# Pairs of the contraction index in the first loads, and a new written-out order of the units, in a fused two-attention kernel

## The chip, the cores and the metric

The kernel runs on one core of one Trainium2 chip. The metric is device time in microseconds (us), the median of several runs. TensorE (PE) does the matrix products, ScalarE (ACT) and VectorE (DVE) move results out of the accumulator banks (PSUM) and do pointwise work, GpSimd (POOL) does masks and copies, and SyncE (SP) issues all DMAs of the program, one after the other.

## The reference

Two attention layers read the same x of 2048 tokens by 512, and a gate mixes them:

```python
g = sigmoid((x * gate_w).sum(-1, keepdims=True))
a = _A_ref(x, mem0, Wq, Wk, Wv, Wo, 32)   # 64 segments of 32 tokens, one after the other
b = _B_ref(x, wq, wk, wv, wo, beta)       # 4 blocks of 512 tokens, 32 heads of 16
return g * a + (1 - g) * b

# _A_ref, for each segment s: 32 heads of 128
h = concatenate([mem, x_segment])         # 8 memory rows and 32 tokens
q, k, v = h @ Wq, h @ Wk, h @ Wv
p = softmax(where(mask, q k^T * scale, -1e9))
o = (p v) @ Wo
mem = o[:8]; outs.append(o[8:])           # the next segment needs mem

# _B_ref, for each block s of one head
o = sg * (phi(q) M / (phi(q) z + 1e-6)) + (1 - sg) * softmax(q k^T * scale + mask) v
M += phi(k)^T v; z += sum of phi(k)
```

## The kernel before, in words

**First stage (0 to about 51 us).** `plan_warm` runs `WARM` = 9 matmuls on zeros (line 509). `plan_loads` requests x in 8 DMAs of 256 KB, the three 512 KB weights of layer B, then small tensors. `x_chunk` turns x with PE transposes (line 573; x is the stationary operand) and copies the result from PSUM into `xT` (helper `evac`, lines 390 on ACT and 392 on DVE). `b_projections` makes layer B's K, Q and V for three of the four blocks (lines 678, 696) and stores them to scratch memory (line 654). Between its pieces, every third piece requests a quarter (1 MB) of layer A's Wk, Wq, Wv. Contraction index 128c+p lies on partition p in chunk c, so a DMA packet of x or of a B weight is one row of 512 bf16, 1 KB. `gate_parts` turns the gate weight with one more transpose.

**Second stage.** `plan_a` runs 16 groups of four segments. A group has a list of units written out in the file (`A_LIST0` to `A_LIST15`); the lists set the order of the instructions on every engine's queue, and all queues are in order. Units of segment r (0 to 3):

- `r.K0x r.K0y` (and Q, V; head half 0 or 1): two halves of a projection, 8 matmuls each on four row groups of the array (line 1281). `r.k0` copies it out, `r.TK0` turns it on DVE.
- `r.S0` scores (lines 1542, 1547), `r.X0` exp on ACT, `r.Y0` mask, `r.M0` sums (line 1577), `r.L0` logarithm and exp on ACT (the reciprocal; lines 1584, 1587), `r.N0` and `r.n0` multiply (lines 1591, 1597), `r.PV0 r.PL0` p times v (lines 1607, 1619), `r.E0a r.E0b` copy out.
- `r.W0a` to `r.W1b`: output projection with Wo (line 1365), 8 matmuls each. `r.H0 r.H1` copy out as float32 (`WF`), `r.F0 r.F1` fold and turn with small float32 matmuls (`fold`, line 1383; the stationary operand is 32 columns of `WF`), `r.hm0 r.hm1` write the memory rows for the next segment, `r.ax0 r.ax1` the token rows to `aT_st`.
- The last 8 tokens of each segment ("left" tokens) of a group are projected together: `KL0x KL0` and so on for the next group, with a prefix `i` for the first group itself. When both V halves are copied out (`VL0e`, `VL1e`, or `iVL0e iVL1e`), `turn_values` stores them to scratch (line 1316) and reads them back in four DMAs that wait for that store (line 1321); `r.PL0` needs them.
- Layer B's attention: `bS` scores (line 909), `bE` exp on ACT with a mask on POOL, `bP` p times v (line 962), `bT` the rest. Layer B's fourth block is projected late: `pj` is half a projection (line 813), `pp` copies out and stores (line 840). After the fourth of the V tiles is projected (the eighth `pj`), four slices of B weights are requested (line 789).
- `wl` requests an eighth of Wo, 512 KB (line 549): two of them for each of `W0a`, `W0b`, `W1a`, `W1b`.
- `of`, `tb`, `tf`: the tail of each group; `tf` turns token rows back with matmuls into PSUM (line 1482).
- A unit's copy goes to ACT or DVE by the table `A_ENG`; a `~` behind the unit swaps the two.

A unit that needs a PSUM bank takes one of eight; it waits until that bank's last reader is done.

## Time and profile before

| what | value |
|---|---|
| median of 3 runs | 845.19 us (843.88 to 845.63) |
| profiled execution, device time | 845.43 us |
| its span, first to last instruction | 843.4 us |
| PE busy | 811.5 us, 96% |
| ACT, DVE, POOL busy | 589.8, 572.0, 284.8 us |
| mean granted PE clock | 0.996 |

The span is the program itself; 2.03 us of the profiled execution lie around it. A chain of waits is read from the top down: start, length, and the engine or DMA that the next piece waited for. In lists of instruction groups the mean of one is its latency, and the busy time counts overlapping ones once.

### The profile page before, as it was taken

Reading aid. Unit: us, or ns where it says so; the run is one execution under the profiler, and the core shown is the slowest. Engines: PE = TensorE matmul, PEld = TensorE weight load, DVE = VectorE, ACT = ScalarE, POOL = GpSimd, SP = SyncE. Lnnn points to the kernel's source line nnn. Section 1 sums busy time; section 2 is a strip of 40 time slices with the busy share of each in tenths; the row PEclk is TensorE's granted clock in tenths of the full one; section 3 lists DMA queues with packets and bytes.
Section 4 is the critical chain, followed back from the end, with each engine's and each line's share of the span. In section 5 each row is a group of like instructions: output and inputs, shape, how many; then the busy total and the mean of one; then the engine's idle time right before and its main releaser. Section 6 shows DMA issues by size and latency. Waiting matters only on the chain.

```text
span 843.4 us, 49436 instructions
## 1 busy us (share of the span) xinstructions
PE 811.5 (96%) x22174; PEld 441.1 (52%) x22174; DVE 572.0 (68%) x1381; ACT 589.8 (70%) x1506; POOL 284.8 (34%) x780
## 2 busy tenths in 40 slices
PE   8997999999999999999999999999999999999997
PEld 4643455555555555555555555555655555555564
DVE  3554457577566767767767777778687787677764
ACT  5545677767777777777677777777767677777544
POOL 3612233333333343333333333333333333434110
PEclk9999899999999999999999999999999999999999
DMA  9996312112002011111012021111112021110111
GB/s 314 419 365 210 73 51 57 54 29 50 28 18 55 24 48 33 46 38 43 19 37 54 20 52 32 47 38 33 36 24 63 18 52 32 36 45 13 33 41 47
DMA packets 84442, 57.50 MB, mean 68 GB/s; under 512 B 55296, under 2 KB 79112, under 8 KB 82696
## 3 DMA queue, kind: packets, MB, share of 16 engines
q1 hardware_dynamic: 84232, 54.36, 21.2%
q8 instruction: 174, 2.85, 1.4%
q14 instruction: 36, 0.29, 0.1%
HBM read 37.14 MB, written 17.20 MB: 64 GB/s over the span
## 4 chain that ended last, share of the span: by engine, by line
PE 85%; ACT 6%; DMA 5%; DVE 2%; issue 1%; SPq 1%; DVEq 0%; POOL 0%; ACTq 0%
PE ps L1281 46%; PE ps L1365 17%; PE ps L1383 3%; PE ps L1607 3%; PE ps L909 2%; PE ps L962 2%; DMA scr_kqd<-stgk 2%; PE ps L1460 2%; PE ps L1542 2%; PE ps L678 1%; PE ps L1577 1%; ACT R_sb L1587 1%; ACT PT L930 1%; DMA Wo_sb<-in_A_Wo_dram 1%; PE ps L813 1%
## 5 line engine op out<-in xcount | busy, mean ns | idle before, releaser
L936 POOL TENSOR_SCALAR_AFFINE_SELECT PT<-PT 128x128 bf16<-128x128 bf16 (+2 forms) x320 | 117.5, 367 | 206.0 <-ACT PT L930 157.7
L930 ACT ACTIVATE PT<-ps 128x512 bf16<-128x512 f32 x320 | 174.9, 610 | 5.4 <-PE ps L909 4.2
L1281 PE MATMUL ps<-Wq_sb,hT 128*32 128x512 bf16 x2048 | 138.1, 383 | 0.4
L1281 PE MATMUL ps<-Wv_sb,hT 128*32 128x512 bf16 x2048 | 138.2, 379 | 0.0
L1281 PE MATMUL ps<-Wk_sb,hT 128*32 128x512 bf16 x2048 | 136.1, 380 | 0.4
L1365 PE MATMUL ps<-Wo_sb,OT_sb 128*32 128x512 bf16 x2048 | 129.9, 381 | 3.9 <-DMA Wo_sb<-in_A_Wo_dram 3.3
L1597 POOL TENSOR_TENSOR P_sb<-P_sb,R_sb 128x64 bf16<-128x64 bf16 x128 | 50.8, 397 | 136.9 <-ACT R_sb L1587 131.1
L390 ACT ACTIVATE OT_sb<-ps 128x320 bf16<-128x320 f32 x170 | 68.7, 435 | 21.8 <-PE ps L1619 20.4
L1281 PEld LDWEIGHTS ps<-Wq_sb,hT 128*32 128x32 bf16 x2048 | 59.1, 97 | 47.0 <-ACT hT L390 2.9
L1281 PEld LDWEIGHTS ps<-Wk_sb,hT 128*32 128x32 bf16 x2048 | 59.4, 97 | 45.8 <-ACT hT L390 2.6
L390 ACT ACTIVATE WF<-ps 128x256 f32<-128x256 f32 x105 | 35.2, 381 | 58.7 <-PE ps L1365 56.4
L1365 PEld LDWEIGHTS ps<-Wo_sb,OT_sb 128*32 128x32 bf16 x2048 | 48.2, 96 | 48.5 <-ACT OT_sb L390 7.5
L1293 DVE STREAM_TRANSPOSE KT_sb<-KN_sb 128x256 f32<-128x256 f32 x128 | 56.5, 441 | 22.2 <-ACT KN_sb L390 19.2
L1293 DVE STREAM_TRANSPOSE QT_sb<-QN_sb 128x256 f32<-128x256 f32 x128 | 56.4, 441 | 22.0 <-ACT QN_sb L390 18.4
L390 ACT ACTIVATE QN_sb<-ps 128x512 bf16<-128x512 f32 x78 | 46.9, 604 | 34.0 <-PE ps L1281 33.3
L390 ACT ACTIVATE KN_sb<-ps 128x512 bf16<-128x512 f32 x75 | 45.0, 602 | 33.2 <-PE ps L1281 32.8
L1556 ACT ACTIVATE P_sb<-ps 128x224 bf16<-128x224 f32 x128 | 45.9, 359 | 28.5 <-PE ps L1547 20.6
L1281 PEld LDWEIGHTS ps<-Wv_sb,hT 128*32 128x32 bf16 x2048 | 50.2, 95 | 23.8 <-issue 0.6
L1591 DVE TENSOR_TENSOR P_sb<-P_sb,R_sb 128x160 bf16<-128x160 bf16 x128 | 42.0, 329 | 20.8 <-ACT R_sb L1587 18.6
L392 DVE CAST V_sb<-ps 128x512 bf16<-128x512 f32 x76 | 51.8, 682 | 5.5 <-PE ps L1281 5.1
L392 DVE CAST OT_sb<-ps 128x320 bf16<-128x320 f32 x86 | 41.1, 487 | 18.7 <-PE ps L1619 17.6
L1607 PEld LDWEIGHTS ps<-P_sb,V_sb 32*128 32x128 bf16 x2048 | 23.4, 91 | 57.6 <-DVE P_sb L1591 26.0
(142 smaller groups left out, 1490.0 us busy)
## 6 DMA issues: line engine op xcount, KB each, us to landing
Wk_sb<-in_A_Wk_dram SPq DMA_DIRECT2D x4, 1024.0 KB, 10.1
Wq_sb<-in_A_Wq_dram SPq DMA_DIRECT2D x4, 1024.0 KB, 13.6
Wv_sb<-in_A_Wv_dram SPq DMA_DIRECT2D x4, 1024.0 KB, 15.4
Wo_sb<-in_A_Wo_dram SPq DMA_DIRECT2D x8, 512.0 KB, 5.7
scr_vld<-VNL SPq DMA_DIRECT2D x16, 256.0 KB, 2.8
VL<-scr_vld SPq DMA_DIRECT2D x64, 64.0 KB
scr_kqd<-stgk SPq DMA_DIRECT2D x12, 256.0 KB, 9.7
Vj<-scr_vd SPq DMA_DIRECT2D x32, 68.0 KB, 2.4
```

Of the source, the lines that this page charges most:

```text
L390: P.op("act", lambda a: a.activation(dst, src, ACT.Copy), reads=[v.rbank[k] for k in bks], writes=dres, name=name)
L392: P.op("dve", lambda d: d.tensor_copy(dst, src), reads=[v.rbank[k] for k in bks], writes=dres, name=name)
L930: P.op("act", lambda a: a.activation(pt, v.pb[bk], ACT.Exp, scale=v.SCALE_B), reads=[v.rbank[bk]], writes=[rp], name="be%d_%d" % (n, t))
L936: P.op("gp", lambda g: g.affine_select(mv, mv, [[0, len(cut)], [1, 128]], ALU.is_ge, 0.0, base=0, channel_multiplier=-1), reads=[rp], writ ...
L1281: ins = pe.matmul(pb[bk][SEG * j:SEG * (j + 1), :], lhs(c), cols(w, j) if split else w[:, 512 * j:512 * (j + 1)], start=(c == 0), stop=(c ...
L1293: P.op("dve", lambda d: d.transpose(to, src), reads=reads, writes=writes, name=name)
L1365: ins = pe.matmul(pb[bk][SEG * j:SEG * (j + 1), :], lhs(4 * k + j), Wo_sb[:, 4 * k + j, :], start=(first and k == ks[0]), stop=False, skip ...
L1383: ins = pe.matmul(pb[bk][SEG * j:SEG * (j + 1), SEG * n:SEG * (n + 1)], part[:, o:o + SEG], v.fold[:, :], start=True, stop=True, skip_grou ...
L1556: P.op("act", lambda a: a.activation(P_sb[:, b, :], pb[bk][:, 0:224], ACT.Exp, scale=SCALE), reads=[rbank[bk]], writes=[Rs("P%d" % b), Rs( ...
L1591: P.op("dve", lambda d: d.tensor_tensor(wide(P_sb, b)[:, :, 0:L], wide(P_sb, b)[:, :, 0:L], R_sb[:, b, :].rearrange("p (i q) -> p i q", q= ...
L1597: P.op(ENG["n"], lambda d: d.tensor_tensor(left(P_sb), left(P_sb), grp04(R_sb[:, b, :]), ALU.mult), reads=[Rs("R%d" % b)], writes=[Rs("P%d ...
L1607: ins = pe.matmul(pb[bks[j]][:, L * i:L * (i + 1)], V_sb[SEG * j:SEG * (j + 1), b, i * E:(i + 1) * E], P_sb[SEG * j:SEG * (j + 1), b, LW * ...
```

## The change

In x, the B weights, A's weights, `gate_w` and the folded outputs, contraction index 256h+2p+n now lies on partition p in chunk 2h+n. A partition then holds two neighbouring rows, and a packet of a B weight is 2 KB; x comes in 2 KB packets (first chunk) or 4 KB packets (the others, one DMA each in place of two). Rows of A's weights stay 8 KB. Operands that run along this index take every second element (`by_pairs`, `a_rows`): the stationary operand of the x transposes and of the folds, the stationary operand and the PSUM destination of `tf`'s matmuls, and the destination of the copies to `aT_st` (units `ax` and `of`). Copies into `xT` write every second or fourth element, and the first chunk's two are split between ACT and DVE in another way. The gate weight arrives in its place, without a transpose. V of a B block is stored once for four tiles (4.25 KB packets) in place of four times. The late slices of the B weights take two DMAs each. `WARM` goes from 9 to 7. All sixteen lists are written anew; every list holds the same projections, scores and outputs as before, and only units of layer B and of the tails change lists. The diff, with lists 1 to 15 and the end of list 0 left out:

```diff
@@ -9,7 +9,7 @@
...
 DEV = dict(nseg_limit=None)
-WARM = 9
+WARM = 7
...
@@ -314,7 +314,7 @@
...
     in_p = alloc(esP, ("wkB", [128, C, DM], BF16, 0), ("wqB", [128, C, DM], BF16, 0), ("phK", [128, 4, DM], BF16, 0), ("etmp", [128, 512], BF16, 5),
-          ("bmask", [128, 136], BF16, 0), ("mskT", [128, 2, 8, 2, 2], BF16, 0), ("mem0_sb", [128, DM], BF16, 0), ("gwr_sb", [128, 128], BF16, 0), ("beta_sb", [128, HB], BF16, 0),
+          ("bmask", [128, 136], BF16, 0), ("mskT", [128, 2, 8, 2, 2], BF16, 0), ("mem0_sb", [128, DM], BF16, 0), ("beta_sb", [128, HB], BF16, 0),
...
@@ -367,7 +367,7 @@
...
-        parts = {"mem0_sb": "mem0", "gwr_sb": "gwr", "beta_sb": "beta", "gB_sb": "gB", "omgB_sb": "omgB"}
+        parts = {"mem0_sb": "mem0", "beta_sb": "beta", "gB_sb": "gB", "omgB_sb": "omgB"}
...
@@ -413,7 +413,7 @@
...
             v.late_const()
-        if n >= 36 and n % 2 == 0 and gates:
+        if n >= 38 and n % 2 == 0 and gates:
...
@@ -514,29 +514,30 @@
...
     P, Rs, C, M = v.P, v.Rs, v.C, v.M
-    xsrc = A_x[0].rearrange("(i p) d -> p i d", p=128)
-
...
     def x(k):
+        if k:
+            P.dma(P.group("x%d" % k), lambda s: s.dma_start(v.x_sb[:, 4 * k:4 * k + 4, :], A_x[0, 512 * k:512 * (k + 1)].rearrange("(p i) d -> p i d", i=4)),
+                  writes=[Rs("x_sb%d%d" % (k, h)) for h in range(2)], name="dma_X%d" % k)
+            return
         for h in range(2):
-            o = 4 * k + 2 * h
-            ld("x%d%d" % (k, h), v.x_sb[:, o:o + 2, :], xsrc[:, o:o + 2, :], "x_sb%d%d" % (k, h), "dma_x%d%d" % (k, h))
+            ld("x%d%d" % (k, h), v.x_sb[:, 2 * h:2 * h + 2, :], A_x[0, 256 * h:256 * (h + 1)].rearrange("(p i) d -> p i d", i=2), "x_sb%d%d" % (k, h), "dma_x%d%d" % (k, h))
...
     for nm, dst, src in (("wk", v.wkB, B_wk), ("wq", v.wqB, B_wq), ("wv", v.wvB, B_wv)):
-        ld("b" + nm, dst[:, :, :], src.rearrange("(c p) n -> p c n", p=128), nm + "B", "dma_" + nm)
+        ld("b" + nm, dst[:, :, :].rearrange("p (h n) m -> p h (n m)", h=2), src.rearrange("(h p n) m -> p h (n m)", h=2, n=2), nm + "B", "dma_" + nm)
...
     for fn, res in ((lambda s: s.dma_start(v.beta_sb[:, :], B_beta.rearrange("(o n) -> o n", o=1).to_broadcast([128, v.HB])), "beta"),
-                    (lambda s: s.dma_start(v.gwr_sb[0:C, :], gate_w.rearrange("(c p) -> c p", p=128)), "gwr"),
+                    (lambda s: s.dma_start(v.gw_sb[:, :].rearrange("p (h n) -> p h n", h=2), gate_w.rearrange("(h p n) -> p h n", h=2, n=2)), "gw"),
...
     def weight(grp, dst, src, res, c):
-        P.dma(grp, lambda s: s.dma_start(dst[:, c, :], src[c * 128:(c + 1) * 128].rearrange("p h e -> p (h e)")),
+        P.dma(grp, lambda s: s.dma_start(dst[:, c, :], src.rearrange("(a p n) h e -> a n p (h e)", a=2, n=2)[c // 2, c % 2]),
...
@@ -558,6 +559,21 @@
...
+def by_pairs(ap):
+
+    return Pairs(ap)
+
+
+class Pairs:
+
+
+    def __init__(self, ap):
+        self.ap = ap.rearrange("p (h t n) -> p h n t", h=2, n=2)
+
+    def __getitem__(self, key):
+        return self.ap[key[0], key[1] // 2, key[1] % 2, key[2]]
+
+
...
@@ -570,14 +586,13 @@
...
                     o = (n * C + c) * 128
-                    ins = pe.transpose(v.pb16[bk][:, o:o + 128], v.x_sb[:, i, c * 128:(c + 1) * 128], v.ident[:, :])
+                    ins = pe.transpose(v.pb16[bk][:, o:o + 128], by_pairs(v.x_sb[:, i, :])[:, c, :], v.ident[:, :])
...
         P.op("pe", f, reads=[Rs("x_sb%d%d" % (k, h)), Rs("ident")], writes=[v.rbank[bk]], name="xtr%d_%d" % (k, h))
-        t0 = 128 * tiles[0]
-        dst = v.xT[:, :, t0:t0 + 256].rearrange("p c (n t) -> p n c t", t=128)
+        dst = v.xT[:, :, 512 * k:512 * (k + 1)].rearrange("p c (t n) -> p n c t", n=4)[:, 2 * h:2 * h + 2] if k else v.xT[:, :, 256 * h:256 * (h + 1)].rearrange("p c (t n) -> p n c t", n=2)
...
         for n in range(2):
-            v.evac("dve" if h else "act", dst[:, n, :, :], src[:, n, :, :], [bk], [Rs("xT%d_%d%d" % (k, h, n))], "xev%d_%d%d" % (k, h, n))
+            v.evac("dve" if (n if k == 0 else h) else "act", dst[:, n, :, :], src[:, n, :, :], [bk], [Rs("xT%d_%d%d" % (k, h, n))], "xev%d_%d%d" % (k, h, n))
...
@@ -599,13 +614,6 @@
...
     st = {}
-
-    def weights():
-        bk = BK.take()
-        P.op("pe", lambda pe, bk=bk: pe.transpose(v.pb16[bk][:, 0:C], v.gwr_sb[0:C, :], v.ident[0:C, 0:C]),
-             reads=[Rs("gwr"), Rs("ident")], writes=[v.rbank[bk]], name="gwtr")
-        v.evac("dve", v.gw_sb[:, :], v.pb16[bk][:, 0:C], [bk], [Rs("gw")], "gwev")
-        BK.give(bk)
...
@@ -630,12 +638,12 @@
...
             for c in range(C):
-                ins = pe.transpose(v.pb16[bk][:, c * v.M:(c + 1) * v.M], v.mem0_sb[0:v.M, c * 128:(c + 1) * 128], v.ident[0:v.M, 0:v.M])
+                ins = pe.transpose(v.pb16[bk][:, c * v.M:(c + 1) * v.M], by_pairs(v.mem0_sb[0:v.M, :])[:, c, :], v.ident[0:v.M, 0:v.M])
...
         BK.give(bk)
-    return [weights, memory] + [lambda k=k: dots(k) for k in range(NTT // 4)]
+    return [memory] + [lambda k=k: dots(k) for k in range(NTT // 4)]
...
@@ -698,8 +706,9 @@
...
         v.evac("act", v.V17[:, sb % 2, tt, :, 0:16].rearrange("p (e m) d -> p m e d", e=2), v.pb[bk].rearrange("p (m e d) -> p m e d", e=2, d=16), [bk], [rv], "evv%d_%d" % (sb, tt))
-        store("stv%d" % sb, v.vd[sb, :, tt, :], v.V17[:, sb % 2, tt, :, :].rearrange("p h w -> p (h w)"), [rv, Rs("V17o")], [Rs("vd%d_%d" % (sb, tt))],
-              "stv%d_%d" % (sb, tt))
+        if tt == 3:
+            store("stv%d" % sb, v.vd[sb].rearrange("p t w -> p (t w)"), v.V17[:, sb % 2, :, :, :].rearrange("p t h w -> p (t h w)"),
+                  [Rs("V17_%d_%d" % (sb % 2, t)) for t in range(4)] + [Rs("V17o")], [Rs("vd%d_%d" % (sb, t)) for t in range(4)], "stV%d" % sb)
...
@@ -784,9 +793,11 @@
...
         m, f = self.work[4 + i]
-        src = (v.B_wk if m == "K" else v.B_wq).rearrange("(c p) n -> p c n", p=128)[:, :, 128 * f:128 * (f + 1)]
-        dst = v.woB_sb[:, i % 4, :].rearrange("p (c w) -> p c w", w=128)
-        P.dma(P.group("lw%d" % i, "lw%d" % (i % 4)), lambda s: s.dma_start(dst, src), writes=[Rs("woc%d" % (i % 4))] + ([Rs("wvB")] if i < 4 else []), name="ldc%d" % i)
+        src = (v.B_wk if m == "K" else v.B_wq).rearrange("(h p n) m -> p h n m", h=2, n=2)[:, :, :, 128 * f:128 * (f + 1)]
+        dst = v.woB_sb[:, i % 4, :].rearrange("p (h n w) -> p h n w", h=2, w=128)
+        grp = P.group("lw%d" % i, "lw%d" % (i % 4))
+        for h in range(2):
+            P.dma(grp, lambda s, h=h: s.dma_start(dst[:, h], src[:, h]), writes=[Rs("woc%d" % (i % 4))] + ([Rs("wvB")] if i < 4 else []), name="ldc%d_%d" % (i, h))
...
@@ -1033,214 +1044,213 @@
 
 
 A_LIST0 = """
-    ixl iKL0x iQL0x iQL0 iQL1x iQL1 iKL0 pj iKL1x iKL0e iKL1 wl 0.Q1x 0.Q1y iQL1e pj 0.K0x 0.K0y 0.q1 0.TQ1 iQL0e~ iKL1e~ bS wl bE iVL0x 0.V0x bE 0.V0y bE
-    0.xc bE 0.Q0x 0.v0~ pp 0.Q0y 0.q0 0.TQ0 bS bP wl bP 0.qt 0.k0~ 0.TK0 pj bE pj wl bE 0.S0 0.X0 iVL0 iVL1x iVL1 0.K1x wl 0.K1y iVL0e~ bE 0.Y0 0.M0 pj xl
-    pp 0.k1 iVL1e bE wl 0.L0 wl 0.TK1 bP wl 0.S1 0.X1 bS 0.Y1 bP bE bE pj bE KL0x 0.M1 0.n0 bE 0.L1 pp 0.V1x 0.V1y 1.xc QL0x 0.v1 QL0 QL0e~ QL1x QL1 bP
-    0.N1 VL0x VL0 0.N0 QL1e~ bT 0.n1 KL1x KL1 VL1x VL0e bP KL0 VL1 KL1e~ 0.PV0 0.PL0 pj VL1e~ 0.E0b~ 0.E0a 0.PV1 0.PL1 0.E1a~ 0.E1b~ KL0e 0.W0a 0.W0b bS
-    pj bE bE bE 0.W1a 0.W1b 0.H0 0.F0 0.oL 0.H1 0.F1 0.hm1~ 1.qt 0.hm0 pp 1.Q1x 1.Q1y 1.Q0x 1.Q0y bE 1.q0 1.TQ0 1.K0x 1.q1 1.TQ1 1.K0y 1.k0 1.TK0 1.K1x
...
+    0.K1x 0.K1y 0.K0x pj 0.k1 wl 0.Q1x ixl iQL1x iKL0x iKL0 iQL1 0.Q0x 0.Q0y 0.q0~ 0.K0y wl iQL1e~ iKL0e~ 0.TK1 bS pj 0.Q1y bE bE bE iVL1x wl 0.k0~ 0.TK0
+    bE bS 0.xc bP iVL1 bP 0.q1 0.TQ1 bE bE pp wl bE bE iVL0x iVL0 wl 0.TQ0 iVL0e~ iKL1x iKL1 iKL1e~ iQL0x iQL0 iQL0e xl pj pj wl 0.qt bP KL0x KL0 KL1x pp
+    0.V0x iVL1e wl 0.V0y 0.v0~ KL1 wl 0.S0 VL1x KL0e~ bP 0.X0 VL1 KL1e~ bS pj 0.Y0 bE QL1x QL1 bE bE 0.S1 0.X1 pj bE pj pj bP 0.Y1 0.M1 QL1e~ pp 0.M0 0.L1
+    0.N1 VL0x VL0 0.L0 0.n0 bT 0.V1x 0.V1y QL0x QL0 VL0e~ 1.xc VL1e~ 0.v1~ 0.N0 0.PV0 0.PL0 0.E0b 0.E0a~ QL0e~ bP 0.W0a 0.n1 0.PV1 0.PL1 0.E1b~ 0.E1a~
+    0.oL 1.qt 0.W0b bS bE bE 0.W1a bE 0.W1b 0.H0 0.F0 bE 0.hm0 0.H1~ 0.ax0 0.F1 1.Q1x 1.Q0x 0.hm1~ 1.Q0y 1.q0~ 1.TQ0 1.Q1y pp 1.K0x 1.K0y 1.k0~ 1.TK0
...
     """
...
@@ -1379,14 +1389,18 @@
...
                 for j in range(4):
-                    o = 256 * hf + 128 * n + SEG * j
-                    ins = pe.matmul(pb[bk][SEG * j:SEG * (j + 1), SEG * n:SEG * (n + 1)], part[:, o:o + SEG], v.fold[:, :],
+                    cols = by_pairs(part[:, :])[:, 2 * hf + n, SEG * j:SEG * (j + 1)]
+                    ins = pe.matmul(pb[bk][SEG * j:SEG * (j + 1), SEG * n:SEG * (n + 1)], cols, v.fold[:, :],
...
         return pb[bk][:, 0:2 * SEG].rearrange("p (c t) -> p c t", t=SEG)
+
+    def a_rows(t):
+
+        return t[:, :, :].rearrange("p c t -> p (c t)").rearrange("p (a t c) -> p a t c", a=2, c=2)
...
@@ -1420,7 +1434,7 @@
...
             n = 3 if g == ngrp - 1 else 4
-            dst = aT_st[par][:, :, :].rearrange("p (a c) (r t) -> p a c r t", a=2, t=SEG)[:, :, :, 0:n, SEG - 8:SEG]
+            dst = a_rows(aT_st[par]).rearrange("p a (r t) c -> p a c r t", t=SEG)[:, :, :, 0:n, SEG - 8:SEG]
...
@@ -1441,7 +1455,7 @@
...
         last = g == ngrp - 1
-        rows = aT_st[g % 2] if last else aTg
+        rows = a_rows(aT_st[g % 2] if last else aTg)
...
@@ -1479,7 +1493,7 @@
...
                         q = slice(SEG * j, SEG * (j + 1))
-                        ins = pe.matmul(pb[bk][q, c * 128:(c + 1) * 128], rows[:, c, q], ident[:, :], start=True, stop=True)
+                        ins = pe.matmul(by_pairs(pb[bk][q, :])[:, c, :], rows[:, c // 2, q, c % 2], ident[:, :], start=True, stop=True)
...
@@ -1654,14 +1668,14 @@
...
             if last:
-                dst = aT_st[par][:, :, SEG * r:SEG * (r + 1)].rearrange("p (a c) t -> p a c t", a=2)
+                dst = a_rows(aT_st[par])[:, :, SEG * r:SEG * (r + 1), :].rearrange("p a t c -> p a c t")
...
                 return
-            dst = aT_st[par][:, :, SEG * r:SEG * (r + 1) - M].rearrange("p (a c) t -> p a c t", a=2)
+            dst = a_rows(aT_st[par])[:, :, SEG * r:SEG * (r + 1) - M, :].rearrange("p a t c -> p a c t")
...
```

## The prediction

> **What bounds the kernel.** I read the page first, then windows of time, then the chain of waits.
>
> ```profile
> span 843.4 us, 49436 instructions
> PE 811.5 (96%) x22174; PEld 441.1 (52%) x22174; DVE 572.0 (68%) x1381; ACT 589.8 (70%) x1506; POOL 284.8 (34%) x780
> ...
> PEclk9999899999999999999999999999999999999999
> ```
>
> PE is the bound; only its 31.9 us of idle time, time at a low clock and work added to it can move the end. In the windows of 10 us (columns: length, then busy time of PE, PEld, DVE, ACT, POOL, then granted clock, DMA share, GB/s) idle time and clock loss sit together:
>
> ```profile
> 50.00:60.00 10.00, 9.88 (x176) 4.94 (x176) 5.39 (x12) 3.37 (x7) 1.14 (x4) 1.00 1.01 346
> 60.00:70.00 10.00, 7.88 (x208) 4.03 (x212) 4.23 (x9) 8.02 (x18) 3.81 (x11) 1.00 0.92 300
> 70.00:80.00 10.00, 8.26 (x184) 3.54 (x176) 7.32 (x17) 5.22 (x11) 2.69 (x8) 1.00 0.58 180
> 80.00:90.00 10.00, 7.06 (x104) 2.88 (x108) 1.64 (x4) 2.98 (x7) 1.58 (x4) 0.66 0.52 136
> ```
>
> Summing such windows, PE idles 11.0 us before 100, 14.6 from 100 to 800, 6.3 after. The chain names the cause near 80 (start, length, what):
>
> ```profile
> 65.60 5.72 DMA scr_vld<-VNL
> ...
> 73.88 0.60 SPq L549
> ...
> 75.08 7.29 DMA Wo_sb<-in_A_Wo_dram
> ...
> 82.41 1.07 PE ps L1365 x5
> ...
> 84.69 5.56 PE ps L1281 x63
> ...
> 162.74 3.43 PE ps L1281 x64
> ```
>
> SP stores the first left values at 65.60, waits 5.3 us for them to land, reads them back until 73.84, and only then issues the last three Wo requests, which five others preceded. PE idles 3.26 us before 82.41. Then 63 matmuls take 5.56 us where 64 take 3.43 at full clock: 2.1 us more.
>
> **The start.** (Timeline; the bracket is idle time before.)
>
> ```profile
> 1.26 4.02 PE L509 MATMUL ps<-WF 128*128 128x512 bf16 x9 [1.26 <-DVE WF L503]
> 5.08 1.85 PE L573 MATMUL ps<-ident,Wo_sb 128*128 128x128 bf16 x16
> 7.77 1.04 PE L678 MATMUL ps<-xT,wkB 128*128 128x512 bf16 x4 [0.85 <-DVE xT L392]
> 9.08 1.04 PE L678 MATMUL ps<-xT,wqB 128*128 128x512 bf16 x4 [0.27 <-DMA wqB<-in_B_wq_dram]
> ```
>
> Warm matmuls start 0.43 us apart (PEld rows), so two fewer bring the transposes 0.85 forward, to 4.2. The fastest x transfer took 2.8 us from its issue at 0.81, so x is there. wk landed at 7.3 (issue 1.82 plus 5.5). From 2 to 8 us, with 1 KB packets alone, DMA moved 282 to 336 GB/s; from 20 to 40, mostly 8 KB rows, 415 to 423. The 1 MB up to wk takes about 0.9 less at the higher rate: 6.4, before the first projection is due at 6.9. The copy on DVE loses speed by its 4 or 8 byte steps: from 0.42 (xT copy) to at most 0.69 (the float32 cast of the same shape), but the first chunk is now split over both engines, so I put it at nothing. The wq wait of 0.27 goes. The first 16 transposes took 1.85 us where a later 16 take 1.06: PE was still slow until about 7; a projection that starts sooner may run slow, +0.2. Sum: -0.9 (bounds 0 and -1.3).
>
> Up to 51 us PE is full but for 0.85 in 40 to 50 and 0.72 at 50.05 (waiting for ACT's copy of V, itself late after 2.5 us of waiting for a store of 256 KB that took 15 us to land behind the backlog). 3.6 MB of x and B weights at 415 instead of about 310 GB/s are 2.9 us less DMA time, and V's stores go from twelve to three. I take -0.6 of that idle time (bounds 0 and -1.5). The gate transpose (0.17) goes: -0.1. Together -1.6.
>
> **Group 0.** I add PE time along the lists: 0.43 us per half projection (8 of the 64 matmuls in 3.43), 0.1 to 0.4 for the small units, as the chain shows them. Both lists hold 58.2 us. `iVL1e`, which releases the store, stands at 13.4 before and 13.5 after, and `0.W1b`, the last user of Wo, at 24.6 in both. So the Wo requests do not move by PE time; what changes is SP's queue. Six requests instead of five stand ahead of the store. The first was issued at 57.92, long after its place (3.9 into a list that began at 51.1), because four V stores (3.62 us on SP from 53.78) and MZ's store stood ahead; now one store does, and the backlog is 2.9 us shorter. The six (3.1 MB at the 300 to 340 GB/s of that stretch, 9 to 10 us) should be through by 66. The values' store, issued about 65, lands by 69; reading back takes 2.5; two requests go out by about 72.6. Three took 7.3 from the last issue; two at about 330 GB/s should need 5, so 77.6. `0.W1b` is due at 49.5 + 24.6 + some 3 us of other waits = 77.1. Residual wait: 0.6 (bounds 0 and 3.3). A short wait need not cool the clock. Gain: 3.3 + 2.1 - 0.6 = 4.8.
>
> New waits in group 0: the second `bS` stands at 7.0 and needs four banks; the pending late tile, Q half 1 and VL half 1 hold three, so it takes banks that the four `bE` behind copies on ACT free at about 8.9: near 2 us. PE stands in it with everything behind. Before, the same stretch had 0.8 (a DVE copy), 1.0 (POOL's mask) and 0.4 (a late store's source); I set these against it: 0, bounds -1 and +1.5. The late slices take eight DMAs more on SP, 0.5 us each. Four of these come before group 1's values, whose first reader is a segment away; cover gone, 2 us. I put it at nothing.
>
> **Groups 1 to 15.** The lists are the same work in another order. For each of the 64 segments and both halves I took the PE work between producer and consumer and compared it with the chain between: sums to PV (0.31 + 0.34 + 0.34 and hand-overs, 1.3), PL to W (0.47 + 0.2), W to fold (0.55), fold to the next projection (0.4), projection to scores (0.62 + 0.45 + 0.25), scores to sums (0.9). The shortfalls add up to 30.3 us before and 30.05 after, for groups 1 to 15 26.1 and 26.2; only group 14 (-0.7) and group 15 (+0.7) differ much. Before, 21 us were really idle from 100 on, so the count is of the right size, and says nothing changes: 0, bounds -3 and +3, for the waits on ACT that it leaves out. The last tail still starts after the last `ax1`: 0.
>
> **Operands with steps.** No row shows the folds' float32 columns 8 bytes apart. The nearest has bf16 4 bytes apart (L1542, keys), which loads as fast as contiguous columns:
>
> ```profile
> L1542 PEld LDWEIGHTS ps<-QT_sb,KT_sb 128*32 128x32 bf16 x2048 | 31.9, 95 | 28.2 <-DVE QT_sb L1293 10.5 <-DVE KT_sb L1293 8.2 <-issue 1.2
> L1383 PEld LDWEIGHTS ps<-fold,WF 128*32 128x32 f32 x2048 | 30.9, 111 | 22.4 <-ACT WF L390 9.2 <-DVE WF L392 2.0 <-issue 1.6
> L1482 PE MATMUL ps<-ident,aTg 128*32 128x128 bf16 x240 | 6.3, 219 | 0.3 <-issue 0.3
> ```
>
> I take 0 for the folds; the upper end is a doubled load, 15 ns (30.9/2048) times 2560, 38 us. The x transposes likewise: 0, at most their 4.7 us of loads again. For L1482, whose result now falls on every second float32 of PSUM, rows give 0 to +3.4: 128 columns on four row groups at 0.43 ns a column (from the two L1577 shapes, 42 ns for 96 columns) are 0.21 us a tail, doubled, 16 times. I take 0.
>
> The Trainium skill speaks against this edit (Advanced Engine Details and Errata, PSUM Cachelines): any non-contiguous access pattern "significantly slows down matmuls". No row here shows single elements with gaps; L1577's 64-column form, in runs of eight, runs at full rate.
>
> **Sum.** -1.6 - 4.8 = -6.4 on the profiled 845.43 (span 843.4 and 2.03 around it) is 839.0; the median lies 0.24 lower: 838.8. Bounds of the forecast's own parts: 834 to 843.5.
>
> **Rivals.**
> - *The last Wo requests come no sooner* (0.14). For it: they still queue behind the read-back of the values, at the same place by PE time. Against it: two instead of three, and a shorter backlog. Then only the start and about 1 us are gained: 842.5.
> - *PSUM steps double `tf`* (0.06): 838.8 + 3.4 = 842.2.
> - *The new order loses on ACT and DVE* (0.10), which my count leaves out: `~` moves copies, and a copy behind a row of `bE` (0.5 to 0.6 each) makes PE wait. Place: groups 1 to 15. At 0.6 us a group it costs 9: 847.8; it decides from 0.43 a group on. Against it: ACT is at 70%, DVE at 68%.
> - *The folds' 8 byte steps slow the weight load* (0.07): 160 folds of 16 loads. At 0.1 us a fold, 16 us: 854.8, slower; it decides from 0.04 us a fold (6.4/160). Against it: L1542.
> - *Gains and losses cancel* (0.06), the first two together with a bad half microsecond here and there: 845.
>
> **How the numbers follow.** The forecast has 0.57. About 0.2%, 1.7 us, is what a measurement of this kernel can tell from no change. Faster: 0.57 + 0.14 + 0.06 = 0.77; same 0.06; slower 0.17. The range goes from 832.5, a little under the forecast's own end since the start's idle time could go wholly, to 848, which takes in the order's loss and leaves out the folds' case.
>
> **What would show it.** Right: the first L678 near 6.9; no half clock in 80 to 90; PE's wait for Wo under 1.5 us; three V stores from the first stage in place of twelve; folds' load mean at 111 ns, L1482 at 219; idle time from 100 to 800 between 12 and 18. Wrong: the Wo wait still at 3, a PEld mean of L1383 well above 111, or idle time from 100 on above 24.

## The result and the profile after

The changed kernel is slower by 0.7%: 851.16 us (median of 4 runs, 849.22 to 852.74) against 845.18, ratio 1.0066, interval 1.0044 to 1.0089. The prediction was 838.8, faster. The profiled execution is the fastest of the four (849.22; before 845.43), so its trace shows 4.1 us of span out of some 5.6 by the ratio.

The page of the changed kernel, to be held against the one of before:

```profile
span 847.5 us, 49417 instructions
PE 814.6 (96%) x22165; PEld 439.3 (52%) x22171; DVE 569.8 (67%) x1366; ACT 602.4 (71%) x1520; POOL 285.0 (34%) x780
...
PEclk9999999999999999999999999999999999999999
```

PE is still the bound, and of the 4.1 us it is busy for 3.1 more. The slice at the low clock has gone, as forecast. The windows from 50 to 90 (length; busy PE, PEld, DVE, ACT, POOL; granted clock; DMA share; GB/s) show the half clock of 80 to 90 gone (1.00 instead of 0.66), but PE idle for 1.97 us in 50 to 60, where it idled 0.12 before, and hardly more work done by 90:

```profile
50.00:60.00 10.00, 8.03 (x136) 3.99 (x138) 2.56 (x7) 3.76 (x7) 0.00 (x0) 1.00 1.05 372
60.00:70.00 10.00, 8.73 (x173) 3.79 (x168) 3.73 (x10) 7.16 (x15) 3.66 (x12) 1.00 0.74 246
70.00:80.00 10.00, 8.64 (x228) 3.83 (x220) 4.68 (x13) 7.93 (x19) 3.24 (x7) 1.00 0.55 161
80.00:90.00 10.00, 7.12 (x160) 2.96 (x160) 3.77 (x9) 4.67 (x12) 2.44 (x6) 1.00 0.66 185
```

The chain of waits in the same stretch (start, length, what):

```profile
69.12 5.90 DMA scr_vld<-VNL
75.03 0.53 SPq L1331
...
77.57 0.60 SPq L550
78.22 5.14 DMA Wo_sb<-in_A_Wo_dram
83.40 0.65 PE ps L1375 x8
...
86.51 2.64 DMA scr_vd<-t_sb
89.17 0.63 ACT t_sb L390
89.80 0.48 ACT QN_sb L390
90.32 0.61 PE ps L1291 x8
```

The values are stored at 69.12 instead of 65.60 and the last piece of Wo is there at 83.40 instead of 82.41. PE's wait for it is short (0.74 instead of 3.26) mainly because PE itself comes late. Then a second chain takes over: a store of late values goes out at 86.51, ACT may write `t_sb` again only when it has landed (89.17), and a projection behind ACT's next copy waits until 90.32.

The start (timeline; idle time before in brackets):

```profile
1.26 3.17 PE L509 MATMUL ps<-WF 128*128 128x512 bf16 x7 [1.26 <-DVE WF L503]
4.22 1.62 PE L589 MATMUL ps<-ident,Wo_sb 128*128 128x128 bf16 x16
5.32 1.33 ACT L390 ACTIVATE xT<-ps 128x512 bf16<-128x512 bf16 x2 [3.23 <-PE ps L589]
6.10 1.33 DVE L392 COPY xT<-ps 128x512 bf16<-128x512 bf16 x2 [4.89 <-ACT xT L390]
7.88 1.02 PE L686 MATMUL ps<-xT,wkB 128*128 128x512 bf16 x4 [2.04 <-DMA wkB<-in_B_wk_dram]
9.14 1.89 PE L686 MATMUL ps<-xT,wqB 128*128 128x512 bf16 x4 [0.23 <-DMA wqB<-in_B_wq_dram]
```

The transposes come at 4.22 as forecast, but the first projection starts at 7.88 instead of 7.77: PE now waits 2.04 us for wk, and from 9.14 on four matmuls take 1.89 us instead of 1.04; the granted clock in 10 to 12 is 0.50. List 0 begins at 52.6 instead of 51.1. Only 0.1 us of this is the later projection. The rest is the half clock: from the first projection to list 0 it takes 44.7 us here, 43.3 before, and 43.2 in e6, which has the same loads and no fall of the clock.

The copies into `xT` are slower too. Before, they read:

```profile
6.17 1.08 ACT L390 ACTIVATE xT<-ps 128x512 bf16<-128x512 bf16 x2 [4.09 <-PE ps L573]
6.96 0.76 DVE L392 COPY xT<-ps 128x512 bf16<-128x512 bf16 x2 [5.76 <-PE ps L573]
```

Into every second element one copy now takes 0.73 us on ACT and 0.72 on DVE, instead of 0.59 and 0.42, and DVE's first one begins only when ACT's first one has ended. They are done at 7.43, not far ahead of wk.

The operands with steps (groups: busy, mean ns of one):

```profile
L1393 PEld LDWEIGHTS ps<-fold,WF 128*32 128x32 f32 x2048 | 31.0, 112 | 22.0 <-ACT WF L390 8.8 <-DVE WF L392 2.4 <-issue 1.6
L1496 PEld LDWEIGHTS ps<-ident,aTg 128*32 128x32 bf16 x240 | 6.1, 116 | 2.2 <-issue 0.7 <-DVE V_sb L392 0.2
L1496 PE MATMUL ps<-ident,aTg 128*32 128x128 bf16 x240 | 9.5, 303 | 0.2 <-issue 0.2
```

The folds' 8-byte steps cost nothing (112 ns against 111). The tail's matmuls into every second word of PSUM take 303 ns instead of 219, and their weight loads 116 instead of 96.

To place the differences, the table takes three marks of each trace: the start of the last matmul of unit `W` from `OT_sb` in segments 1 and 59, and the end of the span. All figures are differences to the trace of before (96.34, 791.52, 843.38), and the last two columns are the stretches between the marks. Such a mark of a single execution is uncertain by 2 us and more. Up to segment 1 the change, e2, e5 and e11 run the same instructions and stand between -0.20 and +2.37, and so do e3, e8 and e10, between -0.63 and -2.84: in e2 the clock was at half from 8 to 14 us, in e3 it fell once in 80 to 90 (0.83 there). From segment 1 to 59 the change, e1, e5, e6 and e11 are alike and lose 2.36 to 3.95. So the medians and their ratios decide, and the marks only show where to search.

| kernel | segment 1 | segment 59 | end | 1 to 59 | 59 to end |
|---|---|---|---|---|---|
| the change | -0.05 | +2.59 | +4.13 | +2.64 | +1.54 |
| e1, 9 warming matmuls | +0.74 | +3.10 | +6.78 | +2.36 | +3.68 |
| e2, PSUM in a row, DVE in halves | +2.37 | +4.58 | +6.12 | +2.21 | +1.54 |
| e3, new lists alone | -0.63 | +0.73 | +3.76 | +1.36 | +3.03 |
| e4, loads and pairs alone | +3.54 | +5.32 | +5.40 | +1.78 | +0.08 |
| e5, last list of before | -0.20 | +2.94 | +3.19 | +3.14 | +0.25 |
| e6, 12 warming matmuls | -0.29 | +3.66 | +5.42 | +3.95 | +1.76 |
| e7, three parts mended | -1.34 | +1.47 | +1.03 | +2.81 | -0.44 |
| e8, before with new lists 0 to 2 | -2.84 | -2.98 | -2.78 | -0.14 | +0.20 |
| e9, e8 with two requests a slice | -2.11 | -2.23 | -1.87 | -0.12 | +0.36 |
| e10, e8 with PSUM steps | -2.54 | -0.51 | -0.17 | +2.03 | +0.34 |
| e11, one block of the last list moved | +0.11 | +3.34 | +5.94 | +3.23 | +2.60 |
| e12, before with new lists 3 to 14 | +0.30 | +1.91 | +1.68 | +1.61 | -0.23 |

### The profile page after: what moved, and what is told of

It is laid out like the page before. It is cut to its first block, busy times and chain, and to the rows that moved or that the text cites. A ratio compares the mean times of both kernels' runs of the same rounds, so it can differ in the third digit from the quotient of the medians.

```text
span 847.5 us, 49417 instructions
## 1 busy us (share of the span) xinstructions
PE 814.6 (96%) x22165; PEld 439.3 (52%) x22171; DVE 569.8 (67%) x1366; ACT 602.4 (71%) x1520; POOL 285.0 (34%) x780
## 4 chain that ended last, share of the span: by engine, by line
PE 85%; ACT 6%; DVE 3%; DMA 2%; issue 1%; POOL 1%; SPq 0%; DVEq 0%; POOLq 0%
PE ps L1291 44%; PE ps L1375 17%; PE ps L1393 4%; PE ps L1621 3%; PE ps L920 3%; PE ps L973 2%; PE ps L686 2%; PE ps L1474 2%; ACT PT L941 2%; PE ps L1556 1%; PE ps L1591 1%; PE ps L704 1%; DMA wqB<-in_B_wq_dram 1%; ACT R_sb L1601 1%; PE ps L1496 1%
## 5 line engine op out<-in xcount | busy, mean ns | idle before, releaser
L1291 PE MATMUL ps<-Wq_sb,hT 128*32 128x512 bf16 x2048 | 135.9, 380 | 0.2
L1611 POOL TENSOR_TENSOR P_sb<-P_sb,R_sb 128x64 bf16<-128x64 bf16 x128 | 51.5, 402 | 154.6 <-ACT R_sb L1601 150.7
L390 ACT ACTIVATE OT_sb<-ps 128x320 bf16<-128x320 f32 x180 | 72.0, 434 | 25.6 <-PE ps L1633 23.9
L1291 PEld LDWEIGHTS ps<-Wk_sb,hT 128*32 128x32 bf16 x2048 | 57.4, 97 | 46.1 <-ACT hT L390 3.0
L390 ACT ACTIVATE QN_sb<-ps 128x512 bf16<-128x512 f32 x90 | 54.3, 604 | 29.1 <-PE ps L1291 28.4
L392 DVE CAST V_sb<-ps 128x512 bf16<-128x512 f32 x79 | 53.7, 682 | 2.8 <-PE ps L1291 1.9
L392 DVE CAST KN_sb<-ps 128x512 bf16<-128x512 f32 x51 | 34.5, 676 | 23.2 <-PE ps L1291 23.0
```

The source lines that it names most:

```text
L390: P.op("act", lambda a: a.activation(dst, src, ACT.Copy), reads=[v.rbank[k] for k in bks], writes=dres, name=name)
L392: P.op("dve", lambda d: d.tensor_copy(dst, src), reads=[v.rbank[k] for k in bks], writes=dres, name=name)
L1291: ins = pe.matmul(pb[bk][SEG * j:SEG * (j + 1), :], lhs(c), cols(w, j) if split else w[:, 512 * j:512 * (j + 1)], start=(c == 0), stop=(c ...
L1611: P.op(ENG["n"], lambda d: d.tensor_tensor(left(P_sb), left(P_sb), grp04(R_sb[:, b, :]), ALU.mult), reads=[Rs("R%d" % b)], writes=[Rs("P%d ...
```

## The experiments

Times are medians; a ratio is to the kernel before, run on the same chip beside it (845.52 us for e1 to e4, 845.76 for e5 to e8, 846.47 for e9 to e12), so kernels of different sets are compared by their ratios. 0.1% is 0.85 us.

**e1: nine warming matmuls in the changed kernel.**

```diff
-WARM = 7
+WARM = 9
```

> The changed kernel with WARM back at 9 and nothing else undone. Theory A (its loss is a sum: a colder start, tf's steps in PSUM, and small waits of the new lists): two more warm matmuls shorten PE's idle stretch before the first projection from 2.0 to about 1.2 us, the granted clock of 0.94 and 0.89 in the first 20 us goes back to 1.00, and list 0 starts 1.5 to 2 us sooner: 849 us. Theory B (the new order alone is what costs): the start is absorbed by later waits and the time stays at 851. Theory C (the packets of 2 KB land later and that alone makes the start late): first projection still at 7.9, time within 0.5 of 851.

852.13 us, ratio 1.0078 (1.0052 to 1.0104): nothing gained. The transposes start at 5.08 as before the change, PE still waits 2.06 us for wk, and the clock in 10 to 12 is 0.51. wk simply landed later here, at 8.1.

**e2: the tail's transposes into consecutive words of PSUM.** The step moves to the one DVE operation behind them, which then needs two halves.

```diff
-  pe.matmul(by_pairs(pb[bk][q, :])[:, c, :], rows[:, c // 2, q, c % 2], ident[:, :], ...)
+  pe.matmul(pb[bk][q, c * 128:(c + 1) * 128], rows[:, c // 2, q, c % 2], ident[:, :], ...)
...
-  scalar_tensor_tensor(fin, pb[bk], g, t1)              # one of 512
+  for each half: scalar_tensor_tensor(fin[half, step 2], pb[bk][half], g, t1[half, step 2])
```

> The changed kernel with tf's matmuls writing each chunk contiguously into PSUM; the step of two is taken by the DVE that reads it, in two instructions of 256 columns instead of one of 512. Theory A: the matmul's mean goes from 303 back to 219 ns and its busy time from 9.5 to 6.3 us, PE is the bound there, so 3.4 us come off: 847.8. Theory B: the matmul gets faster and the time does not, since other waits take the place: 851. A DVE that becomes late would show as a wait of PE for it, and less gain than 2 us.

The matmuls are back at 219 ns (6.3 us busy), but the time is 851.36, ratio 1.0074 (1.005 to 1.0097), no better than the change's 1.0066. DVE has more to do for it: 32 operations of 477 ns in place of 15 of 738 and two of 478, 3.2 us more. That this used up the gain is likely and was not tried apart; from segment 1 to 59 the trace loses 2.21, hardly less than the 2.64 of the change. So this run did not show what the PSUM step costs by itself; e10 does.

**e3 and e4: the two halves of the change apart.**

```diff
# e3: the kernel before
-A_LIST0 ... A_LIST15   (before)
+A_LIST0 ... A_LIST15   (of the change)
# e4: the changed kernel
-A_LIST0 ... A_LIST15   (of the change)
+A_LIST0 ... A_LIST15   (before)
```

> The kernel before with the sixteen new lists and nothing else of the change. Theory A: the wait for Wo shrinks from 3.3 to under 1.5 us and the half clock after it goes (4.7 us), the new waits at the head of list 0 cost about 3, groups 1 to 15 cost 0 to 2: 843 to 846. Theory B: the order is what costs, 849 to 851.

> The changed kernel with the sixteen old lists: pairs, longer packets, WARM 7, tf in steps. Theory A: start 1.5 late (2.5 with the clock), tf 3.4 more, the wait for Wo as before: 849 to 851. Theory B: with the old order the time is that of before, 845, or less by what the shorter DMA backlog saves.

New lists alone: 847.66, ratio 1.0032 (1.0015 to 1.0049). Loads and pairs alone: 849.58, ratio 1.0058 (1.0039 to 1.0076). Both lose. In the table the loads lose 3.54 us by segment 1, with PE's wait for Wo still 3.4; the lists are ahead at segment 1, by 0.63 in spite of a fall of the clock there, and lose 3.03 after segment 59.

**e5: the last list of before in the changed kernel.**

```diff
-A_LIST15   (of the change)
+A_LIST15   (before, its leading tf as bT)
```

> The changed kernel with the last group's list (A_LIST15) as before; its leading tf, which has nothing to do here, becomes a bT. Theory (the new last list opens idle places of PE near the end, 1.5 to 2 us between 820 and 828 us that no later work can take up, and in some runs a fall of the clock behind them): 1.5 to 3 us less than the changed kernel, 848.2 to 849.7, and from the end of segment 59 to the end about 51.9 us as before instead of 53.4. Rival (the last group's order is neutral, and what is lost there only shows up there since it was owed by earlier groups): within 0.7 us of the changed kernel, 850.5 to 851.9.

847.71, ratio 1.0016 (1.0005 to 1.0027), 0.5% or 4.2 us better than the change by the ratios, more than expected. In the traces the eight kernels with the last list of before (the kernel before itself among them) need 51.4 to 52.2 us from segment 59 to the end, the six with the new one 53.4 to 55.5. Timeline of PE in the changed kernel, segment 62:

```profile
824.01 0.28 PE L1591 MATMUL ps<-P_sb,onesb 128*32 128x160 bf16 x8 [0.29 <-DVE P_sb L1574]
824.61 0.46 PE L1393 MATMUL ps<-fold,LN_sb 128*32 128x32 f32 x32 [0.32 <-DVE V_sb L392]
825.57 0.28 PE L1621 MATMUL ps<-P_sb,V_sb 32*128 32x40 bf16 x16 [0.49 <-DVE aT_st L392]
...
826.44 0.27 PE L1621 MATMUL ps<-P_sb,V_sb 32*128 32x40 bf16 x16 [0.57 <-ACT OT_sb L390]
```

Four waits for copies on DVE and ACT in 2.5 us; before, the same stretch of segment 62 had one, 0.64 us. In some executions the clock falls behind them. The window in e3 (same list, columns as above):

```profile
825.00:830.00 5.00, 5.00 (x96) 2.30 (x92) 0.79 (x3) 1.39 (x4) 0.40 (x1) 0.72 0.22 53
```

e1 has 0.77 there, the change's own profiled execution 1.00. That fits its times: the mean granted clock over the whole span was 0.998 in its two faster executions (849.22 and 850.65 us) and 0.996 in the two slower ones (851.67 and 852.74), and one more stretch at half clock as long as the one at the start (3.4 us, 8.8 to 12.2) makes 0.002 of such a span. Where in the span the clock fell in the other three is not on record. Where the clock holds there, the new list costs 1.5 to 2.6 us after segment 59; in e3 and e1, where it falls, 3.0 and 3.7.

**e6: twelve warming matmuls in the changed kernel.**

```diff
-WARM = 7
+WARM = 12
```

> The changed kernel with 12 instead of 7 warming matmuls, so that PE works until about 7.3 us and waits for less than 2 us ahead of the first projection. Theory (the wait of 2.0 us and more ahead of the first projection drops the granted clock to a half between 8 and 12 us, which costs about 2 us that nothing later gives back): clock 1.00 in 8 to 14 us, first projection between 7.9 and 8.5, and 1 to 2.5 us less than the changed kernel, 848.7 to 850.2. Rival (the first 50 us wait for loads anyway, so that a slow start is hidden in later waits): the clock holds, list 0 starts no sooner, within 0.7 us of the changed kernel.

The clock holds (1.00 through the first 20 us) and the first two projections run at full speed. Timeline, then PE's waits up to 100 us (total, times, longest):

```profile
7.99 1.04 PE L686 MATMUL ps<-xT,wkB 128*128 128x512 bf16 x4 [1.75 <-DVE xT L392]
8.94 1.04 PE L686 MATMUL ps<-xT,wqB 128*128 128x512 bf16 x4
```

```profile
PE ps L1291 <- ACT QN_sb L390: 2.4, 1, 2.4
...
PE ps L1375 <- DMA Wo_sb<-in_A_Wo_dram: 1.0, 1, 1.0
```

List 0 begins at 51.2, 1.4 us sooner than in the change. By segment 1 only 0.24 is left: the wait behind ACT's copy grew from 1.5 to 2.4, the one for Wo from 0.7 to 1.0. The time is 850.74, ratio 1.005 (1.0035 to 1.0066), by the ratios 1.4 us less than the change, from which it can't be told. The clock loss is real, and list 0 does start sooner; but here a start that is 1.4 us sooner runs into the queue of SP, which needs from 79.59 to 86.80 for the late slices and sends the store behind them at 86.85, no sooner than in the change.

**e8: the kernel before with the new lists in groups 0 to 2 alone.**

```diff
-A_LIST0, A_LIST1, A_LIST2   (before)
+A_LIST0, A_LIST1, A_LIST2   (of the change)
```

> The kernel before with the new lists in groups 0 to 2 alone. Theory (the new order of group 0 to 2 gains, the new lists from group 3 on lose it again): ahead of the kernel before by 1 to 1.8 us at segments 7 to 11 as with all the new lists, and still by as much at the end, 843.7 to 844.7. Rival (being ahead early is only work put off, which the later lists have to do): the lead is gone by segment 23, 845 to 846.

842.81 us (8 runs, 841.44 to 845.92), ratio 0.9966 (0.995 to 0.9982): **faster than both kernels**, and the lead of 2.84 us at segment 1 stays to the end. The chain of its stretch:

```profile
67.84 5.65 DMA scr_vld<-VNL
...
76.06 0.60 SPq L549
76.70 5.35 DMA Wo_sb<-in_A_Wo_dram
82.10 0.64 PE ps L1364 x8
82.76 0.39 ACT WF L390
83.18 0.44 DVE WF L392
83.66 0.33 PE ps L1382 x16
83.99 3.92 PE ps L1280 x72
```

Wo comes 0.3 us sooner than before, PE waits 1.0 for it, no clock falls, and behind it 72 projection matmuls run without a gap. Most of the lead comes behind Wo: from list 0 to Wo's last matmuls it takes 30.8 us instead of 31.3, from there to the mark in segment 1 11.4 instead of 13.9. That the clock holds is not certain with these lists. In e3, which has the same instructions up to there, PE waits longer for Wo, the clock falls behind it, and 0.63 is left of the lead:

```profile
PE ps L1364 <- DMA Wo_sb<-in_A_Wo_dram: 2.1, 1, 2.1
```

The changed kernel has the same lists here too. It reaches list 0 1.3 us later (52.6 against 51.3), Wo's last matmuls 1.3 us later (83.40 against 82.10), and then waits 1.5 at 90.32 where this one does not: 2.8 us, all that separates them at segment 1 (-0.05 and -2.84).

**e9: e8 with two requests for each late slice.**

```diff
-P.dma(grp, dst <- src)
+for h in range(2): P.dma(grp, dst[:, 2 * h:2 * h + 2] <- src[:, 2 * h:2 * h + 2])
```

> The kernel before with the new lists in groups 0 to 2, and each load of a late slice (ldc) as two requests on SP, as the change has it, everything else as before. Theory (part of what group 0 gains is lost to the SP queue: in the changed kernel the four late slices ahead of a store of scr_vd take 5.2 us of issuing instead of 2.1, the store goes out at 85 to 86.5 instead of 81.3, and ACT's next copy into t_sb, and PE's projection behind it, wait for it): the wait of ACT L390 for DMA scr_vd<-t_sb comes back at 1 to 2 us, segment 1 ends 1 to 1.5 us later than with one request each, and 843.8 to 844.5 against 842.8. Rival (the requests are hidden, and the loss there is of the data that land later): no such wait, within 0.4 us of 842.8.

844.62, ratio 0.9981 (0.997 to 0.9992), by the ratios 0.15% or 1.3 us more than e8, though the intervals overlap. SP's queue in e8 and then in e9 (start, length on the queue):

```profile
80.76 0.51 SPq L789 DMA_DIRECT2D woB_sb<-in_B_wq_dram  x1
81.31 1.95 SPq L840 DMA_DIRECT2D scr_vd<-t_sb  x1
```

```profile
82.83 0.98 SPq L791 DMA_DIRECT2D woB_sb<-in_B_wq_dram  x2
83.86 0.47 SPq L842 DMA_DIRECT2D scr_vd<-t_sb  x1
```

The store goes out 2.5 us later with two requests, as the theory has it. The expected wait of ACT for `scr_vd` did not come at 83.86, only at 86.51 in the change, where SP had also begun the slices 2.2 us later (80.92 against 78.77). The expected place was missed: the 0.7 us lost at segment 1 is a wait for Wo of 2.1 instead of 1.0. The second request can't be blamed for that, since e3 waits as long with one request each and Wo's requests stand ahead of the slices on SP. So where the 1.3 us are lost stays open. The wait for `scr_vd` in the change is not owed to its late start alone: e7 begins list 0 at 51.5, and PE waits 1.6 there. The four slices take 2.1 us of SP in e8 and 5.0 in e9, but 5.5 in the change, 7.2 in e6 and 5.4 in e7, whose queue reads:

```profile
79.74 1.24 SPq L800 DMA_DIRECT2D woB_sb<-in_B_wk_dram  x2
...
85.18 1.28 SPq L851 DMA_DIRECT2D scr_vd<-t_sb  x1
```

So the split takes most of the slack, and a later begin and a slower issue the rest. How much each of the two weighs, and why a request takes longer in the changed kernel, was not tried.

**e10: e8 with the tail's transposes into every second word of PSUM,** read back in order by the one DVE operation (743 ns, as before).

```diff
-pe.matmul(pb[bk][q, c * 128:(c + 1) * 128], rows[:, c, q], ident[:, :], ...)
+pe.matmul(pb[bk][q, :].rearrange("p (h t n) -> p h n t", h=2, n=2)[:, c % 2, c // 2, :], rows[:, c, q], ident[:, :], ...)
```

> The kernel before with the new lists in groups 0 to 2, and the tail's 256 transposes writing every second word of PSUM (read back in order by the one DVE operation that follows). Theory (the step alone makes these matmuls 304 ns instead of 219, and PE has nothing to hide it): 3.2 to 3.6 us more of PE in all, 845.5 to 846.4 against 842.8. Rival (PE's longer matmuls fall into waits for DVE and ACT that are there anyway): 304 ns each, but less than 1 us more, 842.8 to 843.8.

846.73, ratio 1.0004 (0.999 to 1.0018), by the ratios 0.38% or 3.2 us more than e8. The group in e8 and in e10:

```profile
L1481 PE MATMUL ps<-ident,aTg 128*32 128x128 bf16 x240 | 6.5, 219 | 0.4 <-issue 0.4
```

```profile
L1481 PE MATMUL ps<-ident,aTg 128*32 128x128 bf16 x240 | 9.5, 303 | 0.2 <-issue 0.2
```

3.0 us of PE here and 0.2 in the last 16 (0.6 instead of 0.4): the time lost is the PE time added. Nothing hides it.

**e11: one block of the new last list moved, in the changed kernel.**

```diff
- 2.S1 2.X1 1.ax1~ ...  2.v0 2.n1 2.N1 of ofe ...  2.PV0 2.PL0 tl tb 2.E0b
+ 2.S1 2.X1 tl 1.ax1~ ...  2.v0 2.n1 tb 2.N1 of ofe ...  2.PV0 2.PL0 2.E0b
```

> The changed kernel with two units of its last list moved: in segment 2 of the last group tl stands behind X1, and tb (16 matmuls of 128x512, 0.9 us of PE that wait for nothing) stands where the list of before has it, between n1 and N1, instead of behind PL0. Theory (the idle 1.7 us of PE between 823 and 828 us is there because this block no longer covers the chain of DVE and ACT copies ahead of PV and PL): the idle there falls below 1 us and 1 to 2 us less than the changed kernel, 849 to 850. Rival (the idle comes from the whole order of the last list, with ACT and DVE late there by 2 to 3 us): within 0.7 us of the changed kernel.

851.02, ratio 1.0048 (1.0032 to 1.0065): by the median as the rival has it, by the ratio 1.5 us less, and not to be told from the change. The idle time stayed: the block now stands at 826.18, and PE waits 0.32 ahead of it, then 0.48 and 0.90 for the copies of ACT and DVE. The missing cover is not the cause; these engines are late there. Which units of the last list make them late stays open.

**e12: the kernel before with the new lists in groups 3 to 14 alone.**

```diff
-A_LIST3 ... A_LIST14   (before)
+A_LIST3 ... A_LIST14   (of the change)
```

> The kernel before with the new lists in groups 3 to 14 alone (A_LIST15 of before, its leading tf as a bT). Theory (the new lists of the middle cost by themselves, by many small waits; all lists cost 2.1 us, those of groups 0 to 2 gain 2.9 and the last costs about 3.6): 1 to 2 us more than the kernel before, 846.5 to 847.5. Rival (the middle is neutral, and what was lost there with all the lists was a lead given back): within 0.6 us of the kernel before.

847.05, ratio 1.001 (0.9998 to 1.0022): by the ratio 0.9 us more, between the theories. The trace loses 1.61 from segment 1 to 59, 1.46 of it in segments 31 to 39, where e3 and the change lose 1.00 and 1.29; but with the lists of before there e8 loses 0.61 as well and e7 1.48. A cost of about 1 us is possible and not shown.

**e7: the changed kernel with three parts mended.**

```diff
-WARM = 7
+WARM = 12
-A_LIST3 ... A_LIST15   (of the change)
+A_LIST3 ... A_LIST15   (before)
# and the tail as in e2
```

> The changed kernel with 12 warming matmuls, the tail's transposes into consecutive words of PSUM (the copy out in two halves with the step on the DVE side), the new lists in groups 0 to 2 alone and the lists of before in groups 3 to 15. Theory (the start, the PSUM steps and the new lists from group 3 on make up the loss between them): first transposes of the tail at 219 ns, and 844 to 846 us, level with the kernel before or up to 1.5 us faster. Rival (the loads in longer runs cost by themselves, by transfers that land later in the first 90 us): 847.5 to 849.5, with the loss there by 100 us.

845.99, ratio 1.0001 (0.999 to 1.0012), level with the kernel before. It has the lists of e8 and is 0.35% or 3.0 us behind it: 1.5 by segment 1, with the wait behind ACT's copy still 1.6, and 2.95 from there to 59. That stretch holds the DVE halves (3.2 us more of DVE) and copies into `aT_st` with steps (ACT's 128x48: 230 ns against 212 in e8). These two were not tried apart, and kernels alike in that stretch differ by up to 1.6.

By ratio the pieces add up roughly: lists 0 to 2 -2.9 us (e8), lists 3 to 14 +0.9 (e12), list 15 +4.2 (the change against e5), together +2.2, where e3 measured +2.7; PSUM steps +3.2 (e10), two requests +1.3 (e9), the start +1.4 (the change against e6), together +5.9, where e4 measured +4.9. Both halves make +7.6 and the change +5.6; the intervals, about 2 us wide on either side for the change, don't settle whether the halves overlap.

## Why the prediction was wrong, point by point

Four terms failed, each by 2 us or more. Two were put at 0: the last group's list, which costs 4.2 us by the ratios, and the PSUM steps, 3.2. The start was put at -1.6 and lost 1.5, and group 0 was put at -4.8 and gave 2.8 at best.

- **Start, forecast -1.6; it lost 1.5 us by the beginning of list 0.** The first failed step is the rate of the longer packets. From 2 to 8 us the windows move 278, 286 and 330 GB/s with 2 KB packets, 282, 291 and 336 with 1 KB. The rate of 415 was read from another stretch, with 8 KB rows, and laid on these. So wk, forecast for 6.4, landed at 7.7 (in all traces 5.5 to 6.1 us after its issue with 1 KB packets; with 2 KB 5.8 to 6.5, and once, in e7, 4.6), and the two warming matmuls taken away became waiting. "The first L678 near 6.9" read 7.88. The copies into `xT`, put at nothing and at most 0.69 each, took 0.72 on DVE and ended at 7.43, so 6.9 was out of reach even with wk there; in e6 and e7 it is they that end PE's wait. The second failed step is the clock's price, +0.2 for a PE that was still slow: the clock fell after the wait, and that cost about 1.4. Seven traces have the first projections at half rate and reach list 0 at 52.2 to 54.1, the seven others at 50.5 to 51.5. The terms for the mid-stage idle time and the gate transpose (-0.7) gave 0.1 in e6 and 0.5 in e7, by the time from the first projection to list 0.
- **Group 0, forecast -4.8; with the loads of before it gave -2.84 at segment 1 (e8), with those of the change 1.5, just what the start had lost.** Right in this trace: "no half clock in 80 to 90" and "PE's wait for Wo under 1.5" (0.74), and two requests behind the read-back instead of three. Of the two terms the clock's 2.1 came (2.5 in e8, behind Wo). The 2.7 for the wait did not: PE reached Wo's last matmuls only 0.5 us sooner, counted from list 0. Wrong in size: the values' store was put at 65 and came at 69.12, its wait at 4 and took 5.90, the last Wo piece at 77.6 and was there at 83.40 (by its own figures the residual wait is 0.5, not 0.6). A short wait for a transfer can mean that the transfer is early or that the reader is late; here it was the reader. Part of PE's 3.3 us became waits at 59 and 61, forecast as near 2 us (2.0 in the trace) and set against three waits of before.
- **The late slices' eight requests, put at nothing.** The step "whose first reader is a segment away" named the wrong victim. Behind them on SP stands also the store that frees `t_sb`, and ACT, then PE, wait for that: 1.9 and 1.5 us. The eight extra requests alone, on the kernel before, made the store late and no such wait (e9).
- **Groups 1 to 15, forecast 0 from a count of shortfalls (30.3 and 30.05).** Idle time from 100 to 800 was 13.75 us, inside the 12 to 18 named, and whether groups 3 to 14 cost anything (0.9 by e12's ratio) is not settled. It failed in the last group, which it had marked with +0.7 and which costs 4.2 by the ratios, 1.5 to 3.7 in the traces: the count left out how the copies queue on ACT and DVE. This is the rival "the new order loses on ACT and DVE", right in its mechanism and wrong in its place: not 0.6 us in each group but most of it in one.
- **Folds, forecast 0:** right, 112 ns. **PSUM steps, forecast 0 out of 0 to +3.4:** wrong; the upper end held. The row chosen for 0 (L1577 in runs of eight) has no single words with gaps between them. The trace agrees here with the Trainium skill (Advanced Engine Details and Errata, PSUM Cachelines), which warned of it without a number: 219 to 303 ns, 3.2 us in all.
- **V's stores** went from twelve to three in the first stage as forecast (the one at 54.47 took 1.60 us of SP instead of 3.62). The first three Wo requests went out 1.3 us sooner for it (56.59), but the next three stand behind the late store at 65.45, and the gain ends there.

## What to carry to other kernels

When a transfer is made into longer runs, take its new rate from rows of the same stretch and queue; if none are there, the rate of before is the likeliest, and work that was removed because the data "come sooner" turns into waiting. A request that is split adds its issue time to everything behind it on that queue, stores that free a buffer included, so follow each of them to the engine that reuses the buffer. A rewritten order should be tried list by list: here three lists gain 2.9 us, one loses 4.2, and the sum hides both. And a place found in one trace should be held against a second trace with the same instructions there: here such pairs differ by 2 us, as the clock falls or holds.

## What the runs showed of the hardware

- Matmuls of 128 columns that write every second float32 of PSUM took 303 ns instead of 219, while float32 stationary columns 8 bytes apart loaded as fast as contiguous ones (112 and 111 ns). The weight loads of these matmuls took 116 ns instead of 96. That goes with the PSUM step and not with the step of the stationary operand: in e10 its columns are contiguous, and it is 116, in e2 and e7 they stand 4 bytes apart and the result is contiguous, and it is 96.
- Copies of 128x512 bf16 from PSUM into every second element of a bf16 tile took 0.72 us on DVE and 0.73 on ACT instead of 0.42 and 0.59; into every fourth element 1.32 and 1.36. The rows of DVE over both kinds, before and after:

```profile
L392 DVE COPY xT<-ps 128x512 bf16<-128x512 bf16 x8 | 3.0, 420 | 6.8 <-PE ps L573 6.7
L392 DVE COPY xT<-ps 128x512 bf16<-128x512 bf16 x8 | 8.7, 1169 | 5.9 <-ACT xT L390 4.9 <-PE ps L589 0.9
```

- Packets of 2 KB moved no more than packets of 1 KB: 1.79 MB in 931 packets against 1.82 MB in 1839 from 2 to 8 us.
- In six kernels a single wait of PE of 2.04 to 3.19 us ahead of the first projection was followed by matmuls at half rate (four in 1.86 to 1.91 us instead of 1.04), in two with a wait of 1.75 and in e3 with 1.80 not. It is no clean bound: e12, with waits of 1.38 and 0.48 close together, fell too, and e8, with 1.26 and 0.89, did not.
